# Layer one's last two token chunks multiplied plainly instead of by seven products, in a fused attention and two-MLP kernel

## The chip, the cores and the metric

One Trainium2 chip, one core. The metric is the device time of one execution in microseconds. The kernel is written in program order for each engine: TensorE (PE), VectorE (DVE), ScalarE (ACT), GpSimd (POOL), and the queue SP that issues the transfers. Each engine runs its instructions in the order in which the program has them.

## What is computed

A decay attention over 2 batches, 8 heads, 768 tokens, 64 channels gives x with 1536 tokens and 512 features. Two MLPs follow, the first with cosine, the second with sigmoid:

```
for b in range(nb):                      # blocks of 64 tokens
    intra = einsum('bhic,bhjc->bhij', qb, kb) * Dmask;  intra = einsum('bhij,bhjd->bhid', intra, vb)
    inter = einsum('bhid,bhde->bhie', qb * lam_pow, kv_state)
    out[:, :, sl] = intra + inter
    kv_state = lam_block * kv_state + einsum('bhsd,bhse->bhde', kb * rev_pow, vb)
x = out.transpose(0, 2, 1, 3).reshape(1536, 512)
h = x @ w_in;   x = (h * cos(h)) @ w_out          # w_in 512 x 2048, w_out 2048 x 512
h = x @ w_in2;  x = (h / (1 + exp(-h))) @ w_out2
```

## The kernel before

Every float32 operand of the MLPs is split into a high part (rounded for PE) and a low remainder, and a product is three matmuls for each 128 rows of depth: high by high, low weight by high x, high weight by low x. `split` (line 120) is one ACT copy for the high part and one subtraction, mostly on POOL, for the low.

The attention runs over six chunks of 128 positions for both batches. Chunks 0 to 3 fill part A of x (512 tokens of each batch), chunks 4 and 5 part B (256 of each). Per layer, `gemm_in` makes h, applies the function and writes g to DRAM (`gd`); `gemm_outs` loads g (`gf`), splits it into gh and gl and multiplies by w_out. There are eight pairs j of 128-column blocks of w_in. For each pair and each part there is one `Quad`: a 2 x 2 block product by the seven products of Winograd's scheme. `product(Q, i)` is six matmuls, with 512 moving columns in part A and 256 in part B. The products accumulate into three PSUM regions, a and b (the tile `cab`) and d. Between them ACT copies a into b (`copy_ab`, line 432), copies b out twice (`copy_u`, u2 and u4, line 436), and DVE adds these to d (`c22`, `c21`, lines 441 and 444) to give the second half of h, the tile h2 (the profile prints h). The seven products need seven units of x and of the weights: some are plain blocks, others sums and differences. `att_x`, `att_t` and `att_l` make those of x from the attention's result (copy xc, differences xt, high parts xah or xbh, low parts xal or xbl). For a pair's weights, `rebias_w` (ACT, line 106) and `convert_w` (DVE, lines 115 and 116, tiles sb and w) turn raw words into float32, `sum_w` makes four sums S on POOL (line 134), and `split_plain` and `split_sums` split them into the tile win.

The function passes for a half of h are `act_n` (ACT), `act_s` (DVE, line 462), `act_sin` (ACT, line 469) and `act_g` (DVE, line 475, then the transfer that writes g). In layer one they work on tiles s.

The order is written by hand. `gemm_in` interleaves the products of one quad with those of the next, and `tasks` places the weight work at numbered points between them; the lists in the last loop hold the numbers. While layer one starts, the last attention chunk runs between the first products: this stretch is called the passage here. At the end of `gemm_in` the output stage begins between the last products: the seam. In the last steps of the program `send` copies a finished 128-row block out of PSUM (DVE, line 674) and issues its transfer; two neighbouring blocks share one PSUM tile.

Of the kernel before, what the change touches and what calls it, by code (L numbers as in the profile page):

```python
# [21 lines left out]
UNITS = 7  # L22

# [16 lines left out]
def tile_decay_attention__two_mlps(  # L40
# [31 lines left out]
    PAIR = 2 * UNITS * 2 * P * 4  # L72
    WOUT = 2 * TB * 4
# [63 lines left out]
    def split_plain(L, j):  # L137
        t = wring[j // 2 % 2].tile([P, 2, UNITS, 2 * P], F32R, name="win")
        win[L, j] = t
        w0, w1 = w32.pop((L, 2 * j, 0)), w32.pop((L, 2 * j + 1, 0))  # L140
        split(t[:, 0, 0:2].rearrange("p u c -> p (u c)"), t[:, 1, 0:2].rearrange("p u c -> p (u c)"), w0)
        split(t[:, 0, 2], t[:, 1, 2], w1[:, 2 * P:])

    def split_sums(L, j):
        t = win[L, j]
        s = sums.pop((L, j))
        for i in range(2):
            u = slice(3 + 2 * i, 5 + 2 * i)
            split(t[:, 0, u], t[:, 1, u], s[:, 2 * i:2 * i + 2])

    def split_out(L, f):
        t = wring[0 if f < 7 else 1].tile([P, 2, TB], F32R, name="wout")
        split(t[:, 0], t[:, 1], w32.pop((L, f, 1)))
        wout[L, f] = t
# [22 lines left out]
    def x_tiles(L, part):  # L177
        if (L, part) not in xt:
            if part == "A":
                xt[L, part] = tuple(xpool.tile([P, UNITS, 2, TB], F32R, tag=n, name=n) for n in ("xah", "xal"))  # L180
            else:
                xt[L, part] = tuple(yring.tile([P, UNITS, 2, HB], F32R, name=n) for n in ("xbh", "xbl"))
# [83 lines left out]
    def att_qdec(c):  # L266
# [3 lines left out]
        qd = ap_2.tile([P, B, NP, P], F32, tag="qd", name="qd")  # L270
# [106 lines left out]
    def att_l(c):  # L377
        h, l, ps, xc, t = xs.pop(c)
        nc.scalar.copy(h[:, 3:7], t)
        engine, x = (nc.gpsimd, xc) if c < CA else (nc.vector, ps)  # L380
        for o, x in ((slice(0, 2), x[:, 0]), (2, x[:, 1, 1])):
            engine.tensor_tensor(out=l[:, o], in0=x, in1=h[:, o].bitcast(F32), op=ALU.subtract)
        late = lambda: nc.gpsimd.tensor_tensor(out=l[:, 3:7], in0=t, in1=h[:, 3:7].bitcast(F32), op=ALU.subtract)
        if c == CA:
            return late
        late()


    class Quad:
        def __init__(self, L, j, part):  # L390
            self.L, self.j, self.part = L, j, part
            self.n = TB if part == "A" else HB
            self.at = 0 if part == "A" else 2 * TB

    ORDER = [(0, "A"), (1, "A"), (0, "B"), (1, "B")] + [(j, p) for j in range(2, FP - 2) for p in "AB"]
    ORDER += [(FP - 2, "A"), (FP - 1, "A"), (FP - 2, "B"), (FP - 1, "B")]
    quads = [
        [Quad(L, *x) for x in ORDER]
        for L in range(2)
    ]  # L400

    def product(Q, i):
        wu, xu, bank, start = PRODUCTS[i]
        if i == 1:
            n = quads[Q.L].index(Q)
            Q.cab = (ps_c if n % 3 else ps_e).tile([P, 2, TB], F32, tag="cab", name="cab", bufs=2 if n % 3 else 1)
            Q.d = (ps_c if n % 2 else ps_e).tile([P, TB], F32, tag="d", name="d", bufs=1)
            Q.banks = {"a": Q.cab[:, 0, 0:Q.n], "b": Q.cab[:, 1, 0:Q.n], "d": Q.d[:, 0:Q.n]}
            if Q.L == 0 and n < 3:
# [36 lines left out]
    def source(Q, i):  # L446
        return Q.h2 if i else Q.cab[:, :, 0:Q.n]

    def act_n(Q, i):
        Q.s = getattr(Q, "s", {})  # L450
# [20 lines left out]
    def act_g(Q, i):  # L471
# [4 lines left out]
        nc.sync.dma_start(out=gd[Q.L][2 * Q.j + i, :, Q.at:Q.at + 2 * Q.n], in_=t.rearrange("p a c -> p (a c)"))  # L476

    def gemm_in(L, tasks, begun):

        qs = quads[L]  # L480
# [5 lines left out]
        if not begun:  # L486
            late = keep_b()
            late.pop(0)()
            product(qs[0], 1)
            copy_ab(qs[0])  # L490
            product(qs[0], 7)
            late.pop(0)()
            product(qs[0], 6)
            product(qs[0], 2)
            copy_u(qs[0], "u2")
            for i, x in enumerate(late):
                tasks.setdefault(i // 2, []).append(x)
        for n, Q in enumerate(qs):
            nxt = qs[n + 1] if n + 1 < len(qs) else None
            old = qs[n - 1] if n else None  # L500
            if n == len(qs) - 2:
                load_g(L, 0, 0)
# [3 lines left out]
            if old:  # L506
                act_sin(old, 0)
# [6 lines left out]
            if old:  # L514
                act_sin(old, 1)
# [18 lines left out]
            act_s(Q, 0)  # L534
            act_s(Q, 1)
        for i in range(2):
            act_sin(Q, i)
# [19 lines left out]
    def prepare(L, b, f, pieces=1):  # L557
# [3 lines left out]
        if b == 0:  # L561
            if L not in slab:
                slab[L] = [xpool.tile([P, SLOTS, 2, TB], F32R, tag=n, name=m) for n, m in (("xah", "gh"), ("xal", "gl"))]
            gh, gl = (x[:, f % SLOTS] for x in slab[L])
            for i in range(2):
                gt[L, i, f] = gh[:, i], gl[:, i]
                if pieces == 2:
                    split(*gt[L, i, f], t[:, i])
            if pieces == 1:
                split(gh, gl, t)  # L570
# [6 lines left out]
    def y_tiles(L, b):  # L577
        if (L, b) not in ys:
            if b == 1:
                t = ps_e.tile([P, 2, TB], F32, tag="cab", name="y", bufs=1)  # L580
                ys[L, b] = [t, None, t[:, 0], t[:, 1]] + [p.tile([P, TB], F32, tag="d", name="y", bufs=1) for p in (ps_e, ps_c)]
# [304 lines left out]
```

## Time and profile before

| | us |
|---|---|
| median of 3 runs | 614.29 (612.28 to 615.68) |
| the profiled execution | 614.86 |
| its span, first to last instruction | 613.1 |
| PE busy | 572.3 |
| DVE busy | 366.4 |
| POOL busy | 355.2 |
| ACT busy | 305.0 |
| granted TensorE clock, mean | 0.977 |

The page shows busy time by engine and the chain that ended last: 68% of it are PE's instructions. A matmul's end is modelled in this profile, and neighbouring matmuls overlap in it, so the price of one is better read from start to start. The views by stretch show where PE has gaps, and the granted clock of the stretch (1.00 is 2.4 GHz).

### The profile page before, as it was taken

The page shows a single profiled execution, that of the slowest core. Times are in us where ns is not written, and L with a number is a line of the kernel's source. Part 1 is how long each engine was busy: PE and PEld are TensorE (multiplying, and loading weights), DVE is VectorE, ACT ScalarE, POOL GpSimd, SP SyncE. Part 2 cuts the span into 40 slices and gives each one's busy share as a digit, 9 for nine tenths or more (in the row PEclk, how much of TensorE's full clock was granted, in tenths as well). Part 3 has the DMA queues.
Part 4 walks back from the last instruction along what each step waited for, and adds up shares of the span by engine and source line. Part 5 has one row for each costly group of instructions (what it writes and reads, how often), then busy time and mean ns, then how long its engine had stood idle before and what let it go on. Part 6 is the DMA issues. An engine that isn't in the chain of part 4 may idle for free.

```text
span 613.1 us, 8757 instructions
## 1 busy us (share of the span) xinstructions
PE 572.3 (93%) x3312; PEld 474.8 (77%) x3313; DVE 366.4 (60%) x395; ACT 305.0 (50%) x488; POOL 355.2 (58%) x265
## 2 busy tenths in 40 slices
PE   7998598999699699999999999999898999999996
PEld 4887386888578578888887888888787788888884
DVE  5688238688798838950199257667668399302001
ACT  4566347677677836430392265666665455201220
POOL 3687616566492549990269537566745699902450
PEclk9999989999999989999999999999898999999999
DMA  9997215454455857671044017455457877105601
GB/s 177 203 234 181 70 34 192 133 177 155 169 170 178 287 178 283 235 248 34 1 137 138 0 43 237 169 191 190 168 188 247 308 251 242 36 0 192 185 1 69
DMA packets 79227, 97.05 MB, mean 158 GB/s; under 512 B 40785, under 2 KB 57169, under 8 KB 79185
## 3 DMA queue, kind: packets, MB, share of 16 engines
q1 hardware_dynamic: 76944, 95.96, 49.2%
q10 hardware_dynamic: 2240, 0.53, 0.5%
q8 instruction: 26, 0.43, 0.3%
q14 instruction: 17, 0.13, 0.1%
HBM read 68.16 MB, written 28.31 MB: 157 GB/s over the span
## 4 chain that ended last, share of the span: by engine, by line
PE 68%; ACT 7%; DVE 7%; POOL 6%; issue 5%; DMA 5%; ACTq 0%; SPq 0%; POOLq 0%; DVEq 0%
PE y L599 41%; PE cab L414 16%; PE d L414 7%; DMA v<-in_v_dram 2%; DVE s L475 2%; DVE w L116 2%; DVE sb L115 2%; POOL win L122 2%; POOL gl L122 2%; POOL S L134 2%; ACT s L453 1%; DMA q<-in_q_dram 1%; ACT s L469 1%; PE psc L325 1%; ACT s L457 1%
## 5 line engine op out<-in xcount | busy, mean ns | idle before, releaser
L122 POOL TENSOR_TENSOR gl<-gf,gh 128x512 fp32r<-128x512 f32 (+1 forms) x70 | 128.8, 1848 | 94.8 <-ACT gh L121 70.0
L599 PE MATMUL y<-wout,gh 128*128 128x512 f32 x384 | 119.3, 392 | 3.6 <-ACT gh L121 1.8
L599 PE MATMUL y<-gh,wout 128*128 128x512 f32 x384 | 119.7, 393 | 0.6 <-ACT gh L121 0.6
L116 DVE SCALAR_TENSOR_TENSOR w<-w,sb 128x512 uint32<-128x512 uint32 x64 | 92.5, 1446 | 15.2 <-ACT w L106 9.3
L414 PE MATMUL cab<-xah,win 128*128 128x512 f32 x320 | 91.4, 408 | 9.0 <-ACT u L436 5.0
L121 ACT CAST gh<-gf 128x512 fp32r<-128x512 f32 (+1 forms) x70 | 53.5, 775 | 92.7 <-DMA gf<-gd 34.6
L599 PEld LDWEIGHTS y<-wout,gh 128*128 128x128 f32 x384 | 72.0, 188 | 19.4 <-DVE o L674 2.5
L599 PEld LDWEIGHTS y<-gh,wout 128*128 128x128 f32 x384 | 72.6, 190 | 15.8 <-ACT gh L121 0.8
L599 PE MATMUL y<-gl,wout 128*128 128x512 f32 x192 | 75.8, 395 | 2.9 <-POOL gl L122 2.9
L414 PEld LDWEIGHTS cab<-xah,win 128*128 128x128 f32 x320 | 60.0, 196 | 23.2 <-ACT u L436 5.4
L599 PE MATMUL y<-wout,gl 128*128 128x512 f32 x192 | 75.5, 393 | 1.1 <-POOL gl L122 1.1
L134 POOL TENSOR_TENSOR S<-w 128x256 f32<-128x256 f32 x28 | 31.1, 1110 | 71.1 <-DVE w L116 71.1
L122 POOL TENSOR_TENSOR wout<-w,wout 128x512 fp32r<-128x512 f32 x32 | 51.4, 1605 | 32.7 <-ACT wout L121 28.4
L115 DVE TENSOR_SCALAR sb<-raw 128x512 uint32<-128x512 uint32 x64 | 67.1, 1049 | 0.7
L414 PE MATMUL cab<-xbh,win 128*128 128x256 f32 x320 | 53.8, 291 | 8.4 <-ACT cab L432 7.0
L414 PEld LDWEIGHTS cab<-xbh,win 128*128 128x128 f32 x320 | 46.8, 193 | 12.6 <-ACT cab L432 8.5
L122 POOL TENSOR_TENSOR win<-S,win 128x512 fp32r<-128x512 f32 x32 | 48.0, 1520 | 9.7 <-ACT win L121 9.7
L674 DVE COPY o<-y 128x512 f32<-128x512 f32 x12 | 8.1, 690 | 74.7 <-PE y L599 72.1
L436 ACT COPY u<-cab 128x512 f32<-128x512 f32 (+1 forms) x64 | 30.2, 472 | 42.2 <-PE cab L414 42.1
L414 PE MATMUL cab<-xal,win 128*128 128x512 f32 x160 | 50.9, 400 | 0.0
L599 PEld LDWEIGHTS y<-gl,wout 128*128 128x128 f32 x192 | 36.3, 189 | 12.7 <-POOL gl L122 5.3
L106 ACT ACTIVATE w<-raw 128x512 f32<-128x512 f32 x64 | 42.9, 670 | 6.5 <-POOL win L122 6.5
(114 smaller groups left out, 903.0 us busy)
## 6 DMA issues: line engine op xcount, KB each, us to landing
gf<-gd SPq DMA_DIRECT2D x48, 512.0 KB, 4.7
raw<-in_moe_w_in_dram SPq DMA_DIRECT2D x32, 512.0 KB, 3.9
gd<-s SPq DMA_DIRECT2D x32, 512.0 KB, 2.9
raw<-in_moe_w_out_dram SPq DMA_DIRECT2D x32, 512.0 KB, 3.6
gd<-s SPq DMA_DIRECT2D x32, 256.0 KB, 2.0
v<-in_v_dram SPq DMA_DIRECT2D x12, 256.0 KB, 6.0
out_dram<-o SPq DMA_DIRECT2D x12, 256.0 KB, 2.2
k<-in_k_dram SPq DMA_DIRECT2D x6, 256.0 KB, 6.1
```

The source lines that it names most:

```text
L106: nc.scalar.activation(w, raw[piece][:, :, 1].bitcast(F32), AF.Prelu, scale=2.0**-112, alpha=-(2.0**32))
L115: nc.vector.tensor_scalar(out=sb, in0=r[:, :, 0], scalar1=2.0**-29, scalar2=7.0, op0=ALU.mult, op1=ALU.min)
L116: nc.vector.scalar_tensor_tensor(out=w, in0=w, scalar=3, in1=sb, op0=ALU.logical_shift_left, op1=ALU.bitwise_or)
L121: nc.scalar.copy(hi, of)
L122: (engine or nc.gpsimd).tensor_tensor(out=lo, in0=of, in1=hi.bitcast(F32), op=ALU.subtract)
L134: engine.tensor_tensor(out=s[:, i], in0=x, in1=y, op=op)
L325: nc.tensor.matmul(ps[r][:, s, :], kT[half[r], b, s, :], qT[half[r], b, s, :], start=True, stop=True)
L414: nc.tensor.matmul(Q.banks[bank], w[:, part, wu, kt * P:(kt + 1) * P], x[:, xu, kt, :], start=start and m == 0 and kt == 0, stop=m == 2 an ...
L436: nc.scalar.copy(t, Q.banks["b"])
L475: nc.vector.tensor_tensor(out=t, in0=source(Q, i), in1=t, op=ALU.mult)
L599: nc.tensor.matmul(y[m], x, z, start=f == 0 and n == 0, stop=f == FT - 1 and n == 2)
L674: nc.vector.tensor_copy(o, ys[1, b][2 + m])
```

## The change

Part B of layer one is no longer a quad of seven products. `plain(Q, i)` multiplies block i of the pair (128 columns of w_in) by all 512 tokens of part B: twelve matmuls with 512 moving columns, accumulated in one PSUM bank. Chunks 4 and 5 of the attention are stored as they are, high and low, with one copy and one subtraction each. The weights of layer one keep all four plain blocks as units (`WUNITS` is 8). `gemm_in_0` is a new order for layer one: in step j the two plain blocks of pair j - 1 stand between the seven products of pair j in part A. Layer two keeps its quads (`gemm_in_1`).

Other orders change with it. Two pairs' weights and more of the first quads' products stand in the passage. At both seams the first two slices of g are loaded in halves (`load_half`, `load_halves`, `prepare_half`). Four instead of seven w_out blocks are split before the output stage. The PSUM tiles have fixed places (`two_banks`, `one_bank`). In layer two's last steps the row blocks are finished in the order 0, 2, 1, 3.

```diff
+    def plain(Q, i):
+        if i == 0:
+            Q.cab = two_banks(2)
+        w, (xh, xl) = win[Q.L, Q.j], xt[Q.L, Q.part]
+        for m, (part, x) in enumerate(((0, xh), (1, xh), (0, xl))):
+            for kt in range(KT):
+                nc.tensor.matmul(
+                    Q.cab[:, i],
+                    w[:, part, 2 * i + kt // 2, kt % 2 * P:(kt % 2 + 1) * P],
+                    x[:, kt, :],
+                    start=m == 0 and kt == 0,
+                    stop=m == 2 and kt == KT - 1,
+                )
     def att_x(c):
-        part, n = ("A", c) if c < CA else ("B", c - CA)
-        h, l = (x[:, :, :, n * P:(n + 1) * P] for x in x_tiles(0, part))
-        ps = po.pop(c).rearrange("p b (u t) i -> p b u t i", t=2)
+        ps = po.pop(c)
+        if c >= CA:
+            h, l = (
+                x.rearrange("p s (b n i) -> p b n s i", b=B, i=P)[:, :, c - CA] for x in x_tiles(0, "B")
+            )
+            nc.scalar.copy(h, ps)
+            xs[c] = h, l, ps
+            return
     def att_l(c):
+        if c >= CA:
+            h, l, ps = xs.pop(c)
+            nc.vector.tensor_tensor(out=l, in0=ps, in1=h.bitcast(F32), op=ALU.subtract)
+            return
+    def gemm_in_0(tasks):
+        old = quads_a[0]
+        for j in range(1, FP):
+            A, Bq = quads_a[j], quads_b[j - 1]
+            if j > 1:
+                product(A, 1)
+                copy_ab(A)
+                product(A, 7)
+            act_n(old, 1)
+            act_sin(old, 0)
+            act_s(old, 1)
+            act_g(old, 0)
+            product(A, 6)
+            product(A, 2)
+            copy_u(A, "u2")
+            task(j, 0)
+            act_sin(old, 1)
+            act_g(old, 1)
+            plain(Bq, 0)
+            task(j, 1)
+            product(A, 5)
+            copy_u(A, "u4")
+            c22(A)
+            task(j, 2)
+            plain(Bq, 1)
+            act_n(Bq, 0)
+            act_s(Bq, 0)
+            product(A, 3)
+            act_n(A, 0)
+            product(A, 4)
+            c21(A)
+            act_s(A, 0)
+            act_sin(Bq, 0)
+            act_g(Bq, 0)
+            old = A
...
+                for j in range(2, FP):
+                    f = 2 * j
+                    if j > 2:
+                        put((j - 2, 2), *(lambda f=f + i: rebias_w(0, f, 0) for i in range(2)))
+                    for i in range(2):
+                        put((j - 1, 0), lambda f=f + i: convert_w(0, f, 0), load_next)
+                    put((j - 1, 0), lambda j=j: sum_w(0, j, nc.gpsimd))
+                    put((j - 1, 1), lambda j=j: split_plain(0, j))
+                    put((j - 1, 2), lambda j=j: split_sums(0, j))
...
-            for m in range(4):
+            for m in (0, 2, 1, 3):
                 gemm_out(L, 2, FT - 2, (m,))
                 gemm_out(L, 2, FT - 1, (m,))
                 send(2, m)
```

The order of the instructions shows what moved. ACT in the passage, before (win_961 is the weight tile of pair 1, u2_999 and cab_1001 belong to the first two A quads):

```order
L358 COPY xc_838<-pso_796 128x1024
L359 CAST xbh_836<-xc_838 128x4x128
L360 CAST xbh_836<-xc_838 128x2x128
L121 CAST win_776<-S_771 128x512 x2
L106 ACTIVATE w_864<-raw_535 128x512
L379 CAST xbh_836<-xt_866 128x8x128
L432 COPY cab_873<-cab_873 128x512
...
L121 CAST win_961<-S_952 128x512 x2
L379 CAST xbh_836<-xt_973 128x8x128
L436 COPY u2_999<-cab_873 128x512
L432 COPY cab_1001<-cab_1001 128x512
```

The same place after the change:

```order
L362 CAST xbh_843<-pso_796 128x2x4x128
L121 CAST win_776<-S_771 128x512 x2
L459 COPY cab_868<-cab_868 128x512
L106 ACTIVATE w_891<-raw_564 128x512
L121 CAST win_926<-w_815 128x512
L121 CAST win_926<-w_891 128x512
L466 COPY u2_959<-cab_868 128x512
L362 CAST xbh_843<-pso_909 128x2x4x128
L459 COPY cab_977<-cab_977 128x512
L466 COPY u4_993<-cab_868 128x512
L121 CAST win_926<-S_898 128x512 x2
```

The casts from xc and xt are gone from before the bank copies, and the casts of S of pair 1 stand behind the copy u4.

ACT in the middle of layer one after the change, one step of `gemm_in_0` (s_1122 and s_1150 are the two halves of the A quad before):

```order
L459 COPY cab_1135<-cab_1135 128x512
L482 ACTIVATE s_1150<-h2_1091,consts_71 128x1024
L498 ACTIVATE s_1122<-s_1122,consts_71 128x1024
L466 COPY u2_1168<-cab_1135 128x512
L498 ACTIVATE s_1150<-s_1150,consts_71 128x1024
L121 CAST win_1201<-w_1097 128x512
L121 CAST win_1201<-w_1099 128x512
L466 COPY u4_1212<-cab_1135 128x512
L121 CAST win_1201<-S_1180 128x512 x2
L106 ACTIVATE w_1220<-raw_1055 128x512
L482 ACTIVATE s_1236<-cab_1188,consts_71 128x1024
L482 ACTIVATE s_1245<-cab_1135,consts_71 128x1024
```

A step has one bank copy and two copies u, where a pair before had two and four, and the passes on part B (s_1236) have 1024 columns.

SP at the seam of layer one, before (gf_2113 and gf_2144 are the first two slices of g, gf_2222 and gf_2224 the next two; s_2100 and s_2109 are the last A block's halves before the last B block):

```order
L550 DMA gf_2113<-gd0_74 128x1024
L476 DMA gd0_74<-s_2100 128x1024
L92 DMA raw_2140<-in_moe_w_out_dram 128x1024
L550 DMA gf_2144<-gd0_74 128x1024
L476 DMA gd0_74<-s_2109 128x1024
L92 DMA raw_2175<-in_moe_w_out_dram 128x1024
L476 DMA gd0_74<-s_2189 128x512
L550 DMA gf_2222<-gd0_74 128x1024
L550 DMA gf_2224<-gd0_74 128x1024
```

And after (s_1882 is the second half of the last A block, gf_1922 the second halves of slices 0 and 1, s_1919 the last plain block):

```order
L648 DMA gf_1795<-gd0_74 128x512
L648 DMA gf_1797<-gd0_74 128x512
L508 DMA gd0_74<-s_1765 128x1024
L506 DMA gd0_74<-s_1847 128x2x512
L508 DMA gd0_74<-s_1856 128x1024
L92 DMA raw_1895<-in_moe_w_out_dram 128x1024
L92 DMA raw_1900<-in_moe_w_out_dram 128x1024
L508 DMA gd0_74<-s_1882 128x1024
L653 DMA gf_1922<-gd0_74 128x2x512
L639 DMA gf_1924<-gd0_74 128x1024
L639 DMA gf_1926<-gd0_74 128x1024
L506 DMA gd0_74<-s_1919 128x2x512
```

The first halves of slices 0 and 1 are issued four g writes earlier than the second halves, and slice 2 follows the second halves.

## Rows read from the trace of the kernel before

**Rows 1.** Page, part 1: busy us, share of the span, instructions.

```profile
PE 572.3 (93%) x3312; PEld 474.8 (77%) x3313; DVE 366.4 (60%) x395; ACT 305.0 (50%) x488; POOL 355.2 (58%) x265
```

**Rows 2.** Busy time by stretch: from:to, us, engines, granted clock, DMA.

```profile
55.10:87.70 32.60, 24.06 (x151) 17.69 (x150) 11.34 (x21) 14.32 (x24) 16.12 (x13) 0.90 0.21 64
87.70:200.50 112.80, 103.01 (x560) 87.84 (x560) 92.22 (x111) 83.65 (x136) 62.64 (x53) 0.97 0.48 163
200.50:218.70 18.20, 12.67 (x61) 9.98 (x62) 13.08 (x15) 11.11 (x19) 9.30 (x7) 0.83 0.83 287
348.40:468.70 120.30, 117.93 (x655) 102.53 (x654) 81.17 (x101) 73.20 (x132) 66.49 (x58) 0.99 0.48 164
468.70:479.00 10.30, 7.32 (x33) 5.28 (x32) 4.47 (x7) 4.08 (x8) 7.87 (x6) 0.83 1.01 374
479.00:609.10 130.10, 128.47 (x566) 105.53 (x564) 48.94 (x32) 35.17 (x51) 71.08 (x40) 1.00 0.40 137
```

**Rows 3.** PE in order of time: start us, us, instructions, [idle before, releaser].

```profile
118.63 1.07 PE L414 MATMUL d<-xah,win 128*128 128x512 f32 x4
...
119.99 1.07 PE L414 MATMUL cab<-xah,win 128*128 128x512 f32 x4
...
126.90 0.64 PE L414 MATMUL d<-xbh,win 128*128 128x256 f32 x4
...
127.61 0.64 PE L414 MATMUL cab<-xbh,win 128*128 128x256 f32 x4
```

**Rows 4.** PE in order of time, the passage.

```profile
60.04 1.19 PE L414 MATMUL cab<-xah,win 128*128 128x512 f32 x4 [2.10 <-ACT cab L432]
...
76.42 2.07 PE L414 MATMUL cab<-xah,win 128*128 128x512 f32 x4 [5.00 <-ACT u L436]
...
79.15 1.91 PE L414 MATMUL d<-xah,win 128*128 128x512 f32 x4
...
81.71 1.53 PE L414 MATMUL cab<-xah,win 128*128 128x512 f32 x4
```

**Rows 5.** PE's waits, 86 to 206: in total us, times, longest.

```profile
PE cab L414 <- ACT cab L432: 5.1, 4, 3.3
PE d L414 <- DVE h L444: 5.0, 6, 2.1
```

**Rows 6.** ACT in order of time, middle of layer one.

```profile
138.65 0.58 ACT L432 COPY cab<-cab 128x512 f32<-128x512 f32 x1
139.16 1.14 ACT L469 ACTIVATE s<-s,consts 128x1024 f32<-128x1024 f32 x1
140.21 0.35 ACT L436 COPY u<-cab 128x256 f32<-128x256 f32 x1
```

**Rows 7.** DVE in order of time, the same stretch and later.

```profile
140.34 1.23 DVE L475 TENSOR_TENSOR s<-cab,s 128x1024 f32<-128x1024 f32 x1 [0.34 <-ACT s L469]
141.48 0.41 DVE L441 TENSOR_TENSOR h<-d,u 128x256 f32<-128x256 f32 x1
141.81 0.42 DVE L115 TENSOR_SCALAR sb<-raw 128x512 uint32<-128x512 uint32 x1
142.33 0.69 DVE L116 SCALAR_TENSOR_TENSOR w<-w,sb 128x512 uint32<-128x512 uint32 x1
...
149.91 1.52 DVE L115 TENSOR_SCALAR sb<-raw 128x512 uint32<-128x512 uint32 x1
151.53 1.59 DVE L116 SCALAR_TENSOR_TENSOR w<-w,sb 128x512 uint32<-128x512 uint32 x1
```

**Rows 8.** POOL in order of time, the same stretch.

```profile
143.17 1.59 POOL L134 TENSOR_TENSOR S<-w 128x256 f32<-128x256 f32 x1 [6.76 <-DVE w L116]
...
147.40 1.99 POOL L122 TENSOR_TENSOR win<-w,win 128x512 fp32r<-128x512 f32 x2
149.35 3.23 POOL L122 TENSOR_TENSOR win<-S,win 128x512 fp32r<-128x512 f32 x2
```

**Rows 9.** SP's queue, then ACT: loads of g in layer one's seam.

```profile
213.27 0.89 SPq L550 DMA_DIRECT2D gf<-gd  x2
...
220.20 1.14 ACT L121 CAST gh<-gf 128x512 fp32r<-128x512 f32 x2 [5.66 <-DMA gf<-gd]
```

**Rows 10.** PE in order of time, the tail.

```profile
603.73 0.74 PE L599 MATMUL y<-wout,gh 128*128 128x512 f32 x2 [0.79 <-DVE o L674]
```

More of the change, by code (lines that the diff above doesn't have):

```diff
@@ L22 @@
 UNITS = 7
+WUNITS = 8
 PRODUCTS = {
@@ L181, in x_tiles @@
             else:
-                xt[L, part] = tuple(yring.tile([P, UNITS, 2, HB], F32R, name=n) for n in ("xbh", "xbl"))
+                shape = [P, KT, TB] if L == 0 else [P, UNITS, 2, HB]
+                xt[L, part] = tuple(yring.tile(shape, F32R, name=n) for n in ("xbh", "xbl"))
         return xt[L, part]
@@ L377, in att_l @@
     def att_l(c):
+        if c >= CA:
+            h, l, ps = xs.pop(c)
+            nc.vector.tensor_tensor(out=l, in0=ps, in1=h.bitcast(F32), op=ALU.subtract)
+            return
         h, l, ps, xc, t = xs.pop(c)
         nc.scalar.copy(h[:, 3:7], t)
[L380 to L386, printed above, removed]
+        for o, x in ((slice(0, 2), xc[:, 0]), (2, xc[:, 1, 1]), (slice(3, 7), t)):
+            nc.gpsimd.tensor_tensor(out=l[:, o], in0=x, in1=h[:, o].bitcast(F32), op=ALU.subtract)
     class Quad:
@@ L475, in act_g, with task, gemm_in_1 @@
         nc.vector.tensor_tensor(out=t, in0=source(Q, i), in1=t, op=ALU.mult)
-        nc.sync.dma_start(out=gd[Q.L][2 * Q.j + i, :, Q.at:Q.at + 2 * Q.n], in_=t.rearrange("p a c -> p (a c)"))
-    def gemm_in(L, tasks, begun):
-        qs = quads[L]
+        if Q.L == 0 and Q.part == "B":
+            nc.sync.dma_start(out=gd[0][2 * Q.j:2 * Q.j + 2, :, 2 * TB:].rearrange("f p c -> p f c"), in_=t)
+        else:
+            nc.sync.dma_start(out=gd[Q.L][2 * Q.j + i, :, Q.at:Q.at + 2 * Q.n], in_=t.rearrange("p a c -> p (a c)"))
+    def gemm_in_0(tasks):
+        def task(j, i):
+            for x in tasks.get((j, i), []):
+                x()
+        old = quads_a[0]
[32 more added lines that the diff above has]
+            old = A
+        Bq = quads_b[FP - 1]
+        plain(Bq, 0)
+        act_n(old, 1)
+        prepare_half(0, 0, 0)
+        act_sin(old, 0)
+        act_s(old, 1)
+        act_g(old, 0)
+        task(FP, 0)
+        plain(Bq, 1)
+        prepare_half(0, 0, 1)
+        act_sin(old, 1)
+        act_g(old, 1)
+        act_n(Bq, 0)
+        act_s(Bq, 0)
+        load_halves(0)
+        load_g(0, 0, 2)
+        load_g(0, 0, 3)
+        gemm_out(0, 0, 0, (0, 1))
+        task(FP, 1)
+        act_sin(Bq, 0)
+        act_g(Bq, 0)
+        gemm_out(0, 0, 1, (0, 1))
+        prepare_half(0, 1, 0)
+        prepare_half(0, 1, 1)
+        prepare(0, 0, 2)
+    def gemm_in_1(tasks):
+        qs, L = quads, 1
         def task(i):
@@ L484, in task @@
                 x()
[L486 to L497, printed above, removed]
+        late = keep_b()
+        late.pop(0)()
+        product(qs[0], 1)
+        copy_ab(qs[0])
+        product(qs[0], 7)
+        late.pop(0)()
+        product(qs[0], 6)
+        product(qs[0], 2)
+        copy_u(qs[0], "u2")
+        for i, x in enumerate(late):
+            tasks.setdefault(i // 2, []).append(x)
         for n, Q in enumerate(qs):
@@ L555, in load_g, with load_half, load_halves, slabs @@
                 gf[L, 2, f + i] = t[:, i]
-    def prepare(L, b, f, pieces=1):
+    def load_half(L, f):
+        t = tpool.tile([P, TB], F32, tag="t2", name="gf", bufs=5)
+        nc.sync.dma_start(out=t, in_=gd[L][f, :, 0:TB])
+        gf[L, "half", 0, f] = t
+    def load_halves(L):
+        t = tpool.tile([P, 2, TB], F32, tag="t4", name="gf", bufs=4)
+        nc.sync.dma_start(out=t, in_=gd[L][0:2, :, TB:2 * TB].rearrange("f p c -> p f c"))
+        for f in range(2):
+            gf[L, "half", 1, f] = t[:, f]
+    def slabs(L):
+        if L not in slab:
+            slab[L] = [xpool.tile([P, SLOTS, 2, TB], F32R, tag=n, name=m) for n, m in (("xah", "gh"), ("xal", "gl"))]
+        return slab[L]
+    def prepare_half(L, i, f):
+        gt[L, i, f] = tuple(x[:, f % SLOTS, i] for x in slabs(L))
+        split(*gt[L, i, f], gf.pop((L, "half", i, f)))
+    def prepare(L, b, f):
         if f >= FT or (L, b, f) in gt:
@@ L561, in prepare @@
         if b == 0:
[L562 to L564 removed]
+            gh, gl = (x[:, f % SLOTS] for x in slabs(L))
+            split(gh, gl, t)
             for i in range(2):
                 gt[L, i, f] = gh[:, i], gl[:, i]
[L567 to L570, printed above, removed]
         else:
```

173 lines of the change are left out of this document (96 added, 77 removed).

## The prediction

> **What bounds the kernel now.** I read the busy line first: PE 572.3 of 613.1 us, every other engine 60% or less [rows 1]. So the span is PE's work plus PE's losses, and the question is where PE loses. Second view: busy time by stretch, the stretches cut at the seams [rows 2]. Third: PE in order of time, for the price of one product. A product is six matmuls; from one start to the next it takes 119.99 - 118.63 = 1.36 us with 512 moving columns (part A) and 127.61 - 126.90 = 0.715 us with 256 (part B), so 227 and 119 ns a matmul [rows 3]. Setting that work against the stretches of [rows 2] gives the losses:
>
> Passage, 55.1 to 87.7: 11 A products (15.0 us) and about 4.3 us of the last attention chunk in 32.6 us: loss 13.3. Middle of layer one, to 200.5: 45 A and 48 B products, 61.2 + 34.3 = 95.5 in 112.8 us: loss 17.3. Seam into the output stage, to 218.7: 8 B products (5.7) and 12 output matmuls (2.7) in 18.2 us: loss 9.8, with the clock at 0.83. Layer two's product stage: 56 A and 53 B products, 114.1, in 120.3 us: loss 6.2. Its seam, to 479.0: 3 B products and 12 matmuls (4.9) in 10.3 us: loss 5.4. Its output stage is nearly gapless: PE 128.5 of 130.1 us.
>
> The waits inside these: in the passage PE stands 2.10 us for the copy of bank a into b, and 5.00 us for the copy u2, and the two products behind that start 2.73 and 2.56 us apart, 2.6 more than 2 x 1.36: twice the price, so 1.2 instead of 2.4 GHz after the idle time [rows 4], in a stretch with a granted clock of 0.90 [rows 2]. In the middle PE waits for ACT's bank copy (5.1 us) and DVE's h (5.0 us) in many small places [rows 5]; each also delays the restart.
>
> **The change part by part.**
>
> *Part B of layer one, plain.* Out go 56 B products, 56 x 0.715 = 40.0 us. In come 16 half blocks of 12 matmuls with 512 columns, 16 x 12 x 0.227 = 43.5 us. On PE the change costs **+3.5 us**: 192 long matmuls for 336 short ones. The Trainium skill ("TensorE: Matmul & The Clock Gate", Back-to-back issue gap) gives a single warm matmul 262 cycles at 256 columns and 518 at 512; by those figures the exchange would cost 192 x 0.216 - 336 x 0.109 = 4.8 us. The rows charge the short one relatively more, so I keep 3.5.
>
> Beside it go B's bank copies, both u copies, its two h sums, and in the attention the seven-fold x of chunks 4 and 5. B's four half-size function passes become two full-size ones, equal in elements. The weights get 256 more columns to split for each pair.
>
> *Middle.* Each step is now one A and one plain pair, 42 + 24 matmuls x 0.227 = 15.0 us. The waited-for copies now have cover: u2 has 2.7 us of plain work between product 2 and product 5, u4 likewise before product 3, and the bank copy has product 7. What can still bound is a ring through three engines: S done; two casts of S, two rebias, two n passes, one sine, the bank copy, the n pass of h, one sine (ACT); g and two converts (DVE); four S sums (POOL). On ACT a full pass takes 1.05 from start to start and a 512-column copy 0.51 [rows 6]: 5 x 1.05 + 5 x 0.51 = 7.8. DVE: g 1.14 from start to start, two converts alone at 0.42 + 0.69 each, so 3.4 [rows 7]. POOL: the four S sums start at 143.17 and the next kind at 147.40, so 4.2 beside DVE; the first took 1.59, the other three 0.88 each, so 3.5 if all go like those [rows 8]. That is 14.7 to 15.4, and with three or four hand-overs of about 0.1 us the ring is 15.0 to 15.8 us against PE's 15.0. So a step takes 15.0 to 16.0; I take 15.4, because the converts stand where POOL has finished the last pair and S then runs with little DVE beside it. Also POOL's last sub of a pair reaches product 7 about when PE does, with a us or less either way. Seven steps x 0.4: loss 3 against 17.3, **-14.3**.
>
> *Passage.* ACT no longer makes xc, two casts and a cast of xt for chunk 4 ahead of the bank copy, but one cast: the 2.10 us go. Chunk 5's xt, which held u2 for 5.00 us, does not exist any more. Instead product 7 of pair 1 now needs the casts of S, which stand on ACT behind u4, then POOL's sub (3.23 us for two, [rows 8]): PE arrives there some 3.3 us early. Convert 2 stands beside POOL's x work and can take 3.1 us instead of 1.1 [rows 7], which holds the scores by about 0.4 us. I allow 1.3 us for the clock (between nothing and the 2.6 us of [rows 4]) and 1.3 for restarts: loss 6.3 for 13.3, **-7.0** (bounds -4 and -9.5).
>
> *Seam of layer one.* The first two slices of the output stage now come as halves, loaded a step earlier: the first 24 output matmuls (5.5 us) run at once behind the last plain block. But the third slice does not. On SP the load of the second halves and of slice 2 stands behind the g write of the last A block, whose DVE product follows two converts: about 9 us after the last A product. Loads in this place land after 4 to 7 us (issue 213.27, cast 220.20, [rows 9]); then cast, and on POOL 1.25 + 1.25 + 2.4 us. Slice 2 is ready at 19 to 22 us, PE wants it at 11: stall 8 to 10, plus 2.5 us of slow clock. Loss 11.7 for 9.8: **+1.9** (bounds -5 and +4). Here the change gains nothing.
>
> *Seam of layer two.* The first halves are loaded at step 24, so the two waits on gh and gl there go; the second halves and slice 2 come just in time or 1 to 2 us late by the same landing times. Loss 2.0 for 5.4: **-3.4** (bounds 0 and -5). The weights that are no longer split before the seam are split behind it, where POOL was busy 71 of 130 us [rows 2]; no cost.
>
> *Tail.* Column blocks in the order 0, 2, 1, 3: block 1 no longer follows block 0, whose copy out holds the shared tile. There were two such waits, the first with 0.79 us idle [rows 10]; with the restart each costs about 0.95. Now 1.36 us of other matmuls stand there: **-1.9**.
>
> Sum: 3.5 - 14.3 - 7.0 + 1.9 - 3.4 - 1.9 = -21.2. The profiled execution took 614.86 us (span 613.1); its time is 0.6 above the median of 614.29. 614.9 - 21.2 = **593.7 us**.
>
> **The rivals.**
>
> *The ring binds.* S runs beside DVE in every step (4.2 us) and each row's full length counts, without the 0.1 us by which ACT's rows overlap: step 16.3, seven times 0.9 more than in the sum, 6.3: 600. For: DVE and ACT were busy 92.2 and 83.7 of the middle's 112.8 us [rows 2]. Against: that held B's copies, h sums and half-size passes, which go.
>
> *The seam is not late.* If DVE reaches the g of the last A block 3 us sooner and loads land in 4 us, its loss is 5: 587.
>
> *The passage gives back its gain* at product 7 of pair 1, 6 us of wait with a half clock behind: 600.
>
> *Slower: converts beside POOL.* A convert takes 1.1 us alone (0.42 + 0.69 at 141.81) and 3.1 us (1.52 + 1.59 at 149.91) while POOL subtracts [rows 7, 8]. If POOL is still on the last pair when DVE starts both converts, they take 6.2 instead of 2.2, S and POOL are later by that, and the overlap renews itself: 4.0 us a step, 28 us in seven: 622. It decides from 3 us a step. Against: POOL ends a pair some 2.5 us into the step and the converts start at about 5. The Trainium skill ("SBUF — State Buffer", SBUF: two separate sides) states the port pair that DVE and POOL share to be an exclusive lock held for a whole instruction. The trace agrees in kind: 0.42 against 1.52 us.
>
> *Not as told:* the order of the changed program shows the plain blocks where the words say, so I give this nothing.
>
> **How the numbers follow.** Forecast 593.7, 0.60 (its own range 588 to 599). Ring binds, 600: 0.16. Seam early, 587: 0.10. Passage gives back, 600: 0.07. Slower, 622: 0.04. Something of no effect in sum: 0.03. Range 583 to 604: it takes in the early seam with the passage's better bound below, and above the ring with a seam at its worst bound. What a measurement of this kernel tells from no change is about 0.5%, 3 us: faster 0.60 + 0.16 + 0.10 + 0.07 = 0.93, same 0.03, slower 0.04.
>
> **What would show it.** In the changed profile: plain matmuls 227 ns apart; steps of 15.0 to 15.5 us with PE's wait, if any, at product 7 for POOL's win; converts of 1.1 us. No wait of PE over 1 us before product 7 of pair 1, and one of about 3 us there. In layer one's seam an idle PE of 8 to 10 us before the third slice, released by POOL's gl, and 24 output matmuls without wait before it. Layer two's seam with 2 us of waits or less. No wait for o at the end. The forecast is wrong if the steps are over 16.5 us, or if a clock below 2.4 GHz shows in more than the passage and the seam.

## The result and the profile after

The changed kernel took 593.37 us (median of four, 592.26 to 595.52); the kernel before, run beside it, 614.71 (612.28 to 615.68). The ratio is 0.9663, 95% interval 0.9623 to 0.9702. The profiled execution took 592.26 us, its span is 590.5. The forecast of 593.7 and its range held, but several of its terms missed and cancelled each other. One execution of the last kernel below took 618.59 us at a granted clock of 0.85, against 573 to 575 in its five others, and is left out of its ratio.

The page's first part and the views by stretch answer to [rows 1] and [rows 2]; the columns are the same.

```profile
PE 564.3 (96%) x3168; PEld 464.3 (79%) x3168; DVE 347.8 (59%) x355; ACT 295.7 (50%) x440; POOL 350.9 (59%) x261
```

```profile
54.84:78.62 23.78, 20.75 (x151) 15.76 (x149) 10.55 (x13) 10.91 (x18) 13.11 (x11) 1.00 0.21 66
78.62:182.95 104.33, 102.85 (x439) 81.66 (x437) 70.14 (x81) 76.10 (x101) 56.14 (x50) 1.00 0.52 177
182.95:210.12 27.17, 18.70 (x63) 14.29 (x63) 20.02 (x17) 15.83 (x21) 16.17 (x9) 0.81 0.69 243
333.60:453.81 120.21, 116.55 (x655) 101.43 (x654) 77.89 (x96) 72.07 (x130) 66.89 (x58) 1.00 0.48 168
453.81:458.73 4.92, 4.92 (x33) 4.44 (x32) 2.04 (x4) 2.70 (x6) 3.77 (x4) 1.00 1.01 384
458.73:586.60 127.87, 127.87 (x566) 105.64 (x564) 51.23 (x38) 38.70 (x56) 74.71 (x43) 1.00 0.44 149
```

The stretches are the passage (11 A products), the middle (45 A products, 14 plain blocks), layer one's seam (up to full rate), layer two's product stage, its seam and its output stage. Of these stretches layer one's seam alone has a clock below 1.00. PE's waits from the first A product on (total us, times, longest), and last what its weight loads (PEld) wait for in the middle:

```profile
PE cab L703 <- POOL gl L122: 3.9, 2, 2.9
PE cab L445 <- DVE s L504: 3.1, 1, 3.1
PE d L429 <- POOL win L122: 2.7, 2, 1.4
PE cab L429 <- ACT cab L459: 2.4, 3, 1.9
PE cab L703 <- ACT gh L121: 2.4, 1, 2.4
PE d L429 <- ACT win L121: 1.7, 1, 1.7
...
PEld d L429 <- POOL win L122: 4.0, 6, 1.8
```

The u copies, which held PE 5.00 us in [rows 4], are gone from it; so is the copy out at the end. New is the second line, in layer one's seam. PE in order of time, first the passage and a step of the middle, then the seam (start us, us, instructions, [idle before, releaser]):

```profile
70.08 0.73 PE L429 MATMUL d<-xah,win 128*128 128x512 f32 x2 [1.71 <-ACT win L121]
72.13 0.73 PE L429 MATMUL d<-xah,win 128*128 128x512 f32 x2 [1.32 <-POOL win L122]
...
73.17 1.08 PE L429 MATMUL cab<-xah,win 128*128 128x512 f32 x4
...
111.06 2.04 PE L445 MATMUL cab<-xbh,win 128*128 128x512 f32 x8
112.94 1.10 PE L445 MATMUL cab<-xbl,win 128*128 128x512 f32 x4
113.88 1.08 PE L429 MATMUL cab<-xah,win 128*128 128x512 f32 x4
...
122.19 1.34 PE L429 MATMUL d<-xah,win 128*128 128x512 f32 x4
...
126.55 2.04 PE L445 MATMUL cab<-xbh,win 128*128 128x512 f32 x8
```

```profile
186.26 3.52 PE L445 MATMUL cab<-xbh,win 128*128 128x512 f32 x8 [3.14 <-DVE s L504]
189.62 1.10 PE L445 MATMUL cab<-xbl,win 128*128 128x512 f32 x4
...
201.39 0.73 PE L703 MATMUL cab<-gh,wout 128*128 128x512 f32 x2 [2.40 <-ACT gh L121]
205.06 0.79 PE L703 MATMUL cab<-gl,wout 128*128 128x512 f32 x1 [2.94 <-POOL gl L122]
205.65 1.05 PE L703 MATMUL cab<-gh,wout 128*128 128x512 f32 x2
...
206.93 1.06 PE L703 MATMUL cab<-gh,wout 128*128 128x512 f32 x2
```

A plain block takes 113.88 - 111.06 = 2.82 us, so 234 ns a matmul, not 227. A step takes 126.55 - 111.06 = 15.49 us; the five behind the first are 15.5 to 15.6, the first is 16.9. Product 7 is where a step loses time: its four matmuls at 122.19 take 1.34 us, where others take 1.08, while their weight loads wait about 0.4 us for POOL's win. In the seam eight matmuls take 189.62 - 186.26 = 3.36 us behind the new wait (1.88 at 2.4 GHz), and behind the third slice three take 1.28 for 0.68: 1.2 instead of 2.4 GHz for part of each, with a granted clock of 0.81 over the stretch.

### The profile page after: what moved, and what is told of

The parts are those of the page before. It is cut to its first block, busy times and chain, and to the rows that moved or that the text cites. A ratio compares the mean times of both kernels' runs of the same rounds, so it can differ in the third digit from the quotient of the medians.

```text
span 590.5 us, 8374 instructions
## 1 busy us (share of the span) xinstructions
PE 564.3 (96%) x3168; PEld 464.3 (79%) x3168; DVE 347.8 (59%) x355; ACT 295.7 (50%) x440; POOL 350.9 (59%) x261
## 4 chain that ended last, share of the span: by engine, by line
PE 72%; DVE 9%; POOL 6%; issue 4%; DMA 3%; ACT 3%; SPq 1%; ACTq 0%; DVEq 0%; POOLq 0%
PE cab L703 30%; PE cab L429 20%; PE d L429 8%; PE d L703 7%; PE cab L445 6%; DVE xal L122 2%; DVE S L134 2%; POOL win L122 2%; DVE sb L115 1%; DMA q<-in_q_dram 1%; DVE w L116 1%; ACT s L486 1%; DMA v<-in_v_dram 1%; POOL S L134 1%; DMA gf<-gd 1%
## 5 line engine op out<-in xcount | busy, mean ns | idle before, releaser
L703 PE MATMUL cab<-gh,wout 128*128 128x512 f32 x320 | 100.3, 395 | 2.4 <-ACT gh L121 2.4
L703 PE MATMUL cab<-wout,gh 128*128 128x512 f32 x320 | 98.6, 390 | 0.0
L703 PEld LDWEIGHTS cab<-gh,wout 128*128 128x128 f32 x320 | 61.2, 191 | 15.6 <-ACT gh L121 2.8
L703 PEld LDWEIGHTS cab<-wout,gh 128*128 128x128 f32 x320 | 59.9, 188 | 12.1
L703 PE MATMUL cab<-gl,wout 128*128 128x512 f32 x160 | 63.7, 398 | 3.9 <-POOL gl L122 3.9
L703 PE MATMUL cab<-wout,gl 128*128 128x512 f32 x160 | 62.3, 389 | 0.0
L778 DVE COPY o<-cab 128x512 f32<-128x512 f32 x10 | 6.7, 689 | 67.7 <-PE cab L703 65.3
L429 PE MATMUL d<-xah,win 128*128 128x512 f32 x128 | 36.9, 400 | 5.7 <-POOL win L122 2.7
L703 PEld LDWEIGHTS cab<-gl,wout 128*128 128x128 f32 x160 | 30.6, 191 | 11.5 <-POOL gl L122 5.3
L504 DVE TENSOR_TENSOR s<-cab,s 128x1024 f32<-128x1024 f32 (+1 forms) x32 | 34.7, 1084 | 7.0 <-ACT s L486 5.5
```

Of the source, the lines that this page charges most:

```text
L429: nc.tensor.matmul(Q.banks[bank], w[:, part, wu, kt * P:(kt + 1) * P], x[:, xu, kt, :], start=start and m == 0 and kt == 0, stop=m == 2 an ...
L504: nc.vector.tensor_tensor(out=t, in0=source(Q, i), in1=t, op=ALU.mult)
L703: nc.tensor.matmul(y[m], x, z, start=f == 0 and n == 0, stop=f == FT - 1 and n == 2)
L778: nc.vector.tensor_copy(o, ys[1, b][2 + m])
```

## The experiments

All edits are made to the changed kernel. The start of the first A product, up to which nothing differs, lies between 54.8 and 59.1 us in these profiles, so I compare stretches, and medians only beside them.

**The tail.** Row blocks in the old order.

```diff
-            for m in (0, 2, 1, 3):
+            for m in range(4):
```

> The changed kernel with the last column blocks back in the order 0, 1, 2, 3. Theory of the prediction (two waits of PE for the copy out of the block that shares the tile, about 0.95 us each with the restart): 1.9 us slower than the changed kernel, about 595.3 us, with two waits of PE for DVE's o near the end. Rival (the copy out is short enough to be hidden, and the gain of the tail is only what the end of the span shows): within 0.5 us of 593.4, with no such wait or with one of under 0.3 us.

597.33 us; 0.9737 (0.9705 to 0.9769) of the kernel before. PE in order of time, passage and tail:

```profile
73.57 0.73 PE L429 MATMUL d<-xah,win 128*128 128x512 f32 x2 [1.32 <-POOL win L122]
...
74.61 1.91 PE L429 MATMUL cab<-xah,win 128*128 128x512 f32 x4
...
587.72 0.73 PE L703 MATMUL cab<-wout,gh 128*128 128x512 f32 x2 [0.78 <-DVE o L778]
...
591.58 0.73 PE L703 MATMUL cab<-wout,gh 128*128 128x512 f32 x2 [0.84 <-DVE o L778]
```

The two waits are back. From layer two's first output matmul to the last it takes 134.4 us, 132.1 in the changed kernel and 132.2 to 132.8 in the eight other profiles that leave the tail alone: 1.6 to 2.4 us, which is the term of 1.9. The rest of the difference is ahead of the edit, in the profiled execution 1.6 us of it in the passage: the same wait at product 7 as in the changed kernel, but here the four matmuls shown behind it take 1.91 us, not 1.08.

**Layer one's seam.** Three kernels. `seam_bank`: the last pair's plain blocks take the tile that A block 6 has left, and the output stages swap the two tiles. `seam_early`: second halves and half of slice 2 loaded in step 7, splits in the order of use. `seam_both`: both.

```diff
-            Q.cab = two_banks(2)
+            Q.cab = two_banks(0 if Q.j == FP - 1 else 2)
```
```diff
-                put((FP - 1, 0), lambda: load_half(0, 0), lambda: load_half(0, 1))
+                put((FP - 1, 0), *(lambda f=f, i=i: load_half(0, f, i) for f, i in ((0, 0), (1, 0), (2, 0), (0, 1), (1, 1))))
```

> The changed kernel with one thing else: the plain blocks of the last pair write the PSUM tile that the A block before last has left, not the single tile of the plain blocks, and the output stages swap these two tiles. The wait of 3.14 us for DVE's g of the pair before goes, and the slow clock behind it (1.5 us). Theory (the third output slice is late by its own load and splits, whatever PE does before): PE reaches it 4.6 us earlier and waits 4.6 us longer there; time within 1 us of 593.4, the wait before the third slice about 10 instead of 5.3 us. Rival (the wait was a loss of its own): 4.6 us faster, 588.8.

> The changed kernel, where in layer one's seam the second halves of slices 0 and 1 and the first half of slice 2 are loaded together with the first halves, a step earlier, and where the splits stand in the order of their use. The tile of the last plain blocks stays, and so does its wait. Theory (load and splits of the third slice cost 5.3 us of waits and some 3.5 us of slow clock behind them): 8 to 9 us faster than the changed kernel, about 585, with under 1 us of waits at the third slice, and the 3.1 us at the plain block still there. Rival (POOL, not the load, is what is late, since it must make the same splits): 2 to 3 us faster, 591, and PE still waits 2 us or more for POOL's gl.

> Both edits of this seam together. Theory (two waits in a row, the second hidden behind the first): the tile's 4.6 us now count beside the 8 to 9 of the loads: 12 to 13.5 us faster than the changed kernel, about 580.5, PE without a wait over 0.5 us from the last A product to the fourth slice. Rival (the splits on POOL bound the seam): PE waits 3 us or more for POOL's gl at the third or fourth slice, 585 or more.

597.07, 587.09 and 587.57 us; ratios 0.9730 (0.9697 to 0.9763), 0.9575 (0.9535 to 0.9615), 0.9570 (0.9535 to 0.9605). From product 4 of the last A block to layer two's first product the changed kernel takes 333.60 - 181.59 = 152.0 us, these 152.8, 144.8 and 144.3. PE of `seam_bank` in order of time, and PE's waits in the seam of `seam_both`:

```profile
204.75 1.22 PE L703 MATMUL cab<-gh,wout 128*128 128x512 f32 x2 [7.30 <-ACT gh L121]
208.42 0.79 PE L703 MATMUL cab<-gl,wout 128*128 128x512 f32 x1 [2.45 <-POOL gl L122]
```

```profile
PE cab L704 <- POOL wout L122: 1.4, 1, 1.4
PE cab L704 <- DVE s L504: 1.3, 1, 1.3
PE cab L704 <- POOL gl L122: 1.2, 1, 1.2
```

With the tile free, PE does not wait at the plain block and waits 9.75 instead of 5.34 us at the third slice: the new wait costs nothing by itself, since the slice is late anyway. (Its median is 3.7 above the changed kernel's, but the stretch holds 0.8; in its profile a start 1.6 us later and 1.6 us at 1.2 GHz in the passage, both ahead of the edit, hold most of the rest.) The third slice is late as forecast, though the longer part of the wait, 7.30 us, is for ACT's gh and not for POOL's gl. With the loads early, 7.2 us go and no wait for the third slice is left. Both together should have given 12 or more and gave 7.7: now POOL's splits and DVE are late in three places, by 1.2 to 1.4 us each. The time is the rival's (585 or more), but its single wait of 3 us for gl does not stand there. By the medians (587.09 and 587.57) the tile adds nothing to the early loads.

**The passage.** The cast of S ahead of the copy u2.

```diff
+        split_sums(0, 1)
         copy_u(A[0], "u2", True)
...
         c22(A[0])
-        split_sums(0, 1)
```

> The changed kernel, where in the passage ACT casts the sums S of pair 1 before it copies u2, and no longer behind u4. Theory (PE's 3.0 us at product 7 of pair 1 are the order on ACT: the sums were ready at 64.2 and their cast began at 68.9): the wait falls to 0.7 us or less and the kernel is 2.4 us faster, 591.0, since the waits behind it stay. Rival (the next wait takes it up: the first step of the middle waits 1.4 us for the splits of pair 2, which hang on DVE's g and not on PE): 1 us faster or less, with a wait of 3 to 4 us at product 7 of pair 2.

590.75 us, 0.9622 (0.9582 to 0.9661). PE's waits from 56 to 100:

```profile
PE d L429 <- POOL win L122: 1.8, 2, 1.4
```

The passage takes 20.8 for 23.8 us. Product 7 of pair 1 waits 0.35 us, and the 1.4 of the first step are the same as before: no wait takes up the gain.

**The ring.** Sums on DVE.

```diff
-                    put((j - 1, 0), lambda j=j: sum_w(0, j, nc.gpsimd))
+                    put((j - 1, 0), lambda j=j: sum_w(0, j, nc.vector))
```

> The changed kernel, where in layer one the four weight sums S of pairs 2 to 7 are made on DVE behind the converts and not on POOL. Theory (a step of 15.5 us is a ring over ACT, DVE and POOL, closed by POOL's splits at product 7, and PE alone would take 15.2): POOL ends a pair 1 to 2 us earlier, the waits of the d products go, steps of 15.2 us: 2 us faster, and 1.5 us more at the first step: about 590. Rival (DVE is what closes the ring): its extra 1.5 to 3 us delay g and the h sums, steps of 16 us or more, 3 us slower or more.

592.08 us, 0.9660 (0.9606 to 0.9715). Plain blocks of two steps in order of time:

```profile
115.34 2.04 PE L445 MATMUL cab<-xbh,win 128*128 128x512 f32 x8
...
130.54 2.04 PE L445 MATMUL cab<-xbh,win 128*128 128x512 f32 x8
```

Steps of 15.2 us, which is PE's own work (42 x 0.227 + 24 x 0.234 = 15.15); the first is 16.4. The wait of PE's weight loads for POOL's win is gone from the middle. So POOL's splits did close a ring, and it was worth 0.3 us a step, 2.1 us over the middle. The medians can't show that: this one is 1.3 below the changed kernel's, and the ratios, 0.9660 and 0.9663, are the same within their intervals. (The profiled execution took 596.94, the longest of four: its passage, which the edit doesn't touch, took 27.4 us at a granted clock of 0.88.)

**The cover.** Both plain blocks behind product 4.

```diff
-            plain(Bq, 0)
             task(j, 1)
...
-            plain(Bq, 1)
...
             act_s(A, 0)
+            plain(Bq, 0)
+            plain(Bq, 1)
```

> The changed kernel, where the two plain blocks of a step stand behind its product 4 and no longer between products 2 and 5 and between 5 and 3; all work is the same. Theory (plain work is the cover of the copies u2 and u4, which empty the bank that the next product writes): each of the two copies of a step now costs PE 0.8 to 1.1 us, seven steps: 11 to 15 us slower than the changed kernel, 604 to 609, with PE's waits for ACT's u in each step. Rival (the steps are set by the ring over ACT, DVE and POOL and not by the copies, and the waits only move): 593 to 597.

626.64 us, 1.0199 (1.0149 to 1.0250): slower than the kernel before. PE, then ACT, in order of time in one step:

```profile
140.57 1.19 PE L429 MATMUL cab<-xah,win 128*128 128x512 f32 x4 [1.37 <-ACT cab L459]
...
144.26 1.19 PE L429 MATMUL cab<-xah,win 128*128 128x512 f32 x4 [0.68 <-ACT u L466]
...
147.57 1.19 PE L429 MATMUL cab<-xah,win 128*128 128x512 f32 x4 [1.65 <-ACT u L466]
```

```profile
146.41 0.62 ACT L121 CAST win<-w 128x512 fp32r<-128x512 f32 x1 [0.64 <-DVE w L116]
146.94 0.58 ACT L466 COPY u<-cab 128x512 f32<-128x512 f32 x1
```

Steps of 19.75 us, 4.2 more than with cover; I had allowed 1.6 to 2.2. The copies alone don't take that long: u4 stands on ACT behind a cast of weights that waits for DVE's convert, and the bank copy waits too, since the passes of the plain blocks now come late. The plain work hides the queues in front of the copies, not the copies alone.

**The price of a plain matmul.** First a kernel, executed once, in which single pairs differ (pair 4 takes part A's x, `xa`), then a pad ahead of part B's x.

```diff
+        if Q.j == 4:
+            xh, xl = xa
```
```diff
+                yring.tile([P, 8], F32, name="pad")
```

> A plain matmul goes every 234 ns and a product's every 227 ns, with the same 512 columns. Each plain pair of layer one differs here in one thing; the others are as they were. Pair 2: the twelve matmuls of a block go six to each of two banks, as a product's six do. Pair 3: the two halves of the inner dimension one after the other, each over its three parts, in the order of a product. Pair 4: the moving matrix is part A's x and not part B's. Pair 5: the weights are those of the sums. Pairs 2, 4 and 5 compute something else than the reference. If runs of twelve to one bank are the cause, pair 2 goes at 227; if the order, pair 3; if the place of the moving matrix in SBUF, pair 4; if that of the weights, pair 5. If none, all stay at 234 ns. Time as for the changed kernel, within 2 us.

> The changed kernel with part B's x of layer one laid 32 bytes lower in SBUF, so that each row of it begins at a multiple of 64 bytes as part A's x does; now it begins 32 bytes behind one. No instruction is changed. Theory (the 7 ns of a plain matmul come from this offset, since with part A's x as the moving matrix they were gone): plain matmuls go every 227 ns; a step, which is set by the ring, gets shorter by 0.1 us at most, so 0.5 to 1 us faster than the changed kernel. Rival (the place, and not its remainder, or a neighbour's traffic, costs the 7 ns): 234 ns as before, no change.

The first took 595.61 us, the second 595.89, 0.9708 (0.9671 to 0.9745), its first A product at 59.05. Pair 4 of the first, then a block of the second:

```profile
144.08 1.98 PE L455 MATMUL cab<-xah,win 128*128 128x512 f32 x8
145.90 1.07 PE L455 MATMUL cab<-xal,win 128*128 128x512 f32 x4
146.80 1.07 PE L429 MATMUL cab<-xah,win 128*128 128x512 f32 x4
```

```profile
115.23 2.01 PE L446 MATMUL cab<-xbh,win 128*128 128x512 f32 x8
117.08 1.08 PE L446 MATMUL cab<-xbl,win 128*128 128x512 f32 x4
117.99 1.10 PE L430 MATMUL cab<-xah,win 128*128 128x512 f32 x4
```

With part A's x a block takes 2.72 us (227 ns a matmul); pairs 2, 3 and 5 stay at 2.81. So it is the moving matrix. Moved by 32 bytes, to a multiple of 64, it takes 2.76: 230 ns, half of the gap, which neither theory had said. (The addresses are those of the program's layout of SBUF; no row shows them.) Steps stay at 15.5 us although PE has less to do, as they must if the ring sets them.

**Layer two's seam.** Whole slices at the old places.

```diff
-                put(24, *(lambda f=f: load_half(1, f) for f in range(2)))
-                put(28, lambda: load_halves(1), lambda: prepare_half(1, 0, 0))
...
+                for f, (n, m) in enumerate(((28, 29), (28, 30), (30, 31), (30, 32))):
+                    tasks.setdefault(n, []).append(lambda f=f: load_g(1, 0, f))
```

> The changed kernel with layer two's seam as it was before the change: whole slices 0 to 3 loaded at the old places, each split in two halves, no halves loaded at step 24. Theory (the halves loaded early are what removes the waits of this seam, which had 5.4 us of losses before and has none now): waits for gh and gl come back, 3.5 to 5.5 us slower than the changed kernel, 597 to 599. Rival (it is the weights no longer split ahead of the seam, which leave POOL and ACT free, that removed them): under 1.5 us slower, 595 or less.

599.50 us, 0.9773 (0.9739 to 0.9807). PE in order of time:

```profile
457.87 0.73 PE L712 MATMUL cab<-wout,gh 128*128 128x512 f32 x2 [0.77 <-ACT gh L121]
459.22 0.50 PE L712 MATMUL cab<-wout,gl 128*128 128x512 f32 x1 [0.62 <-POOL gl L122]
...
462.16 0.50 PE L712 MATMUL cab<-wout,gl 128*128 128x512 f32 x1 [0.57 <-POOL gl L122]
```

The waits are back. Up to the first output matmul the product stage is 1.0 us longer than in the changed kernel (121.9 for 120.9), the rest takes 134.2 us for 132.1 to 132.8 in the others: 2.4 to 3.2 us, less than expected and more than the rival's 1.5. (The profiled execution took 597.88, 5.6 more than that of the changed kernel. Ahead of the edit its start is 2.7 us later, its passage 1.6 longer and layer one's output stretch 1.9 shorter.) Before, the same seam lost 5.4 with a granted clock of 0.83 [rows 2]; here no matmuls at 1.2 GHz follow. What the fewer split weights did to that was not tried.

**All together.** `best2` joins the edits (both of the seam, the cast, sums on DVE, the 64 bytes), makes pair 2's converts and sums ahead of product 3 of pair 0, and converts output weights 2 and 3 one step earlier. `best3` differs from it in the placement alone, a pad of 96 instead of 32 bytes.

```diff
+        for f in (4, 5):
+            rebias_w(0, f, 0)
+        for f in (4, 5):
+            convert_w(0, f, 0)
+            load_next()
+        sum_w(0, 2, nc.vector)
...
+                for f in (2, 3):
+                    put((FP - 1, 2), lambda f=f: convert_w(0, f, 1), load_next)
```

> All edits together on the changed kernel: the sums of pair 1 cast early, pair 2 converted and summed ahead of the first step, weight sums on DVE, part B's x at a multiple of 64 bytes, the other PSUM tile for the last pair, the early loads of the seam, and in it the converts and splits of output weights 2 and 3 a step earlier. Theory (each loss was a wait of its own): passage 3.0, first step 1.5, six steps of 15.0 for 15.5 us 3.0, seam 11 to 12.5: 575 us, from 573 to 577. Rival (DVE, which now makes sums and converts too, becomes the ring's longest part): steps of 15.5 us or more and 3 us of waits in the seam, 581 or more.

> The kernel with all edits, with one difference: part B's x of layer one now begins at a multiple of 128 bytes; it began 64 bytes behind one there, and 96 behind one in the changed kernel. Plain matmuls went every 234 ns at 96, 230.5 at 64; part A's x and every other moving tile, at multiples of 128, go at 227. Theory (the remainder by 128 sets the price): 227 ns, a plain block of 2.72 us, products between plain blocks of 1.36 instead of 1.39, steps of 15.0 instead of 15.12 us, in all 1 us faster than that kernel, about 574.3. Rival (the place high in SBUF keeps the rest): 230 ns and 15.12 us again, 575.3.

575.34 us, 0.9377 (0.9348 to 0.9406), and 575.27, 0.9359 (0.9327 to 0.9391). A block of `best3`:

```profile
91.69 1.98 PE L446 MATMUL cab<-xbh,win 128*128 128x512 f32 x8
93.50 1.07 PE L446 MATMUL cab<-xbl,win 128*128 128x512 f32 x4
94.41 1.07 PE L430 MATMUL cab<-xah,win 128*128 128x512 f32 x4
```

2.72 us: 227 ns, and steps of 14.96 us, which is 66 x 0.227. In `best2` steps are 15.12. So `best3` has the price of the theory and the time of the rival. From product 4 of the last A block to layer two it takes 140.5 us in `best2` and 141.7 in `best3`, where one wait for a split of output weights is 1.52 us instead of 0.47; that takes up the 1 us which the steps gained. The changed kernel had 152.0 there and `seam_both` 144.3: the converts a step earlier, or POOL without the sums, brought the rest; which of the two was not tried. Both are 18 us faster than the changed kernel.

## Why the prediction was right, and where it wasn't

By stretch, measured change against the forecast term (losses as the prediction defines them):

| term | forecast | measured | |
|---|---|---|---|
| plain for B products | +3.5 | +5.0 | 16 x 2.81 - 40.0 |
| middle | -14.3 | -13.5 | 104.3 - 45 x 1.36 - 14 x 2.81 = 3.8 for 17.3 |
| passage | -7.0 | -8.8 | 23.8 for 32.6 |
| layer one's seam | +1.9 | +3.1 | 27.2 - 14.3 of work = 12.9 for 9.8 |
| layer two's seam | -3.4 | -5.4 | no loss left |
| output and tail | -1.9 | -2.2 | 127.9 for 130.1 |
| all else | 0 | -0.8 | start 0.3, layer one's output 0.3, remainder 0.2 |
| sum | -21.2 | -22.6 | spans 590.5 and 613.1; by the medians -21.3 |

*Plain matmuls.* The step that failed is taking 227 ns from part A's rows [rows 3] for a matrix that lies elsewhere. By the program's layout part B's x begins 96 bytes behind a multiple of 128, and a matmul takes 234 ns; at 64 it takes 230 ns, at 0 it takes 227, with nothing but a pad between the kernels compared. The miss cost the changed kernel little: in `align`, at 230 ns, steps are still 15.5 us. Where the ring is gone the price shows, 15.12 us in `best2` and 14.96 in `best3`. The Trainium skill's figures ("TensorE: Matmul & The Clock Gate", Back-to-back issue gap) gave 4.8 us for the exchange, near the 5.0 found. The agreement is chance: with the x moved, the plain matmuls cost 3.5 more than the old products' 40.0 (16 x 2.72 - 40.0), as the rows say. Whether the old products would gain by a move too was not tried.

*Middle.* Right in kind and nearly in size: steps of 15.5 for a forecast of 15.4. The ring was the bound, by 0.3 us over PE, shown by `sums_dve` and by `align`; its waits stand at product 7 for POOL's win, as said, and add to a longer first step (1.4 us). The rival "the ring binds" was priced at 16.3 and is out. `uncovered` shows that the gain of 13.5 hangs on the order: without it the changed kernel loses 12 us against the one before. No run has the old products of part B in the new order, so what the fewer copies gave and what the longer cover gave stays apart only in argument. One reading of the rows was loose: of the 5.1 us of waits for the bank copy in [rows 5], 3.3 are a single wait and 0.9 stand in the seam; the sum does not use it.

*Passage.* The wait was forecast as 3.3 us and is 3.03 (1.71 + 1.32). The 1.3 us for the clock did not come in the profiled execution, where the granted clock of the passage is 1.00; that and the wait are nearly the whole miss. The step was sound, though: in five experiments that share this code up to there, the passage took 25.4 us (granted clock 0.93) or 27.4 (0.88), with matmuls at 1.2 GHz behind that wait, and in three 23.8 (1.00). `uncovered`, whose passage ends otherwise, shows 1.2 GHz there too. What decides between the two stays open; `cast_early` cuts the wait at product 7 to 0.35 us, and its passage has a clock of 1.00.

*Layer one's seam.* The forecast of 8 to 10 us before the third slice is what `seam_bank` measured, 9.75. What I missed is a wait ahead of it: the last pair's first plain block has no A product in front of it, so the single tile of the plain blocks is still read by DVE's g of the pair before. The prediction had gone through the queues and not through the PSUM tiles, so it put this wait at nothing. The miss cost little, since 4.4 of the 4.6 us came off the wait behind.

*Layer two's seam.* The sign was right, the bound of -5 was passed. The step that failed is "1 to 2 us late by the same landing times": nothing is late there. `l1_undo` ties 2.4 to 3.2 us of it to the halves loaded early; the rest stays open.

*Tail.* Right: 1.6 to 2.4 us by `tail_old`, in two waits of 0.78 and 0.84.

*Slower by converts beside POOL.* It did not come in the steps. DVE in order of time, one step of the changed kernel:

```profile
173.42 0.42 DVE L115 TENSOR_SCALAR sb<-raw 128x512 uint32<-128x512 uint32 x1
173.94 0.69 DVE L116 SCALAR_TENSOR_TENSOR w<-w,sb 128x512 uint32<-128x512 uint32 x1
```

That is the 1.1 us which the forecast named as the sign, the same in all seven steps; the 3.1 us of [rows 7] came with POOL at work. Behind the seam, at 202.82 and 205.39, where POOL subtracts, one pair takes 2.46 + 2.68 us.

The total was nearer than its parts, and that is luck: +1.5, +0.8 and +1.2 stand against -1.8, -2.0, -0.3 and the -0.8 of all else.

## What to carry to other kernels

Work without dependencies is worth most between two steps that wait for each other through another engine; what it hides is the queue ahead of the copy, so moving it elsewhere can cost more than it saves. When several waits stand in a row, ask when the last of them would end if the first were gone: removing the first alone gave nothing here, and removing the second brought up the next. Go through the tiles as well as the queues, and look at where a moving matrix begins.

## What the runs showed that I had not expected

- Where the moving matrix begins changed the price of a float32r matmul with 512 columns: 234 ns at 96 bytes behind a multiple of 128, 230 at 64, 227 at 0 (the changed kernel, `align`, `best3`). These three places are all that was tried. Products of part A between blocks at 234 ns go slower too: 1.39 us instead of 1.36. Whether layer two's shorter matmuls on part B gain by a move was not tried.
- Behind one and the same wait of 3.0 us PE's rows show 2.4 GHz in four profiles and 1.2 in six, worth 1.6 us, in one profile 3.6.
